# Attention and a gated MLP on one core: three edits to the order of work around the first MLP chunks

## The chip, the core and the metric

The kernel runs on one core of one Trainium2 chip. The metric is device time in microseconds, from a timed run of the whole program. The core has TensorE (PE in the profile, with its weight loads as PEld), VectorE (DVE), ScalarE (ACT), GpSimd (POOL) and SyncE (SP), which issues most of the reads from DRAM. Each engine executes its own instructions strictly in the order in which the program was written out for it.

## The reference

One layer of a transformer in float32: layer norm, attention over eight positions at distance two, a residual, layer norm, a gated MLP, a residual. Sequence 2048, model width 576, 32 heads of width 18, hidden width 4608.

```python
x = A_x
h = x + _A_ref(_layernorm(x, axis=-1), A_wqkv, A_wo)
h2 = h + _B_ref(_layernorm(h, axis=-1), B_w_gate, B_w_up, B_w_down)
...
off = jnp.arange(W) * dil                      # W = 8, dil = 2
idx = pos[:, None] - off[None, :]
logits = jnp.einsum("bhsd,bhswd->bhsw", q, kg) * scale
attn = _softmax(jnp.where(mask, logits, -1e9), axis=-1)
o = jnp.einsum("bhsw,bhswd->bhsd", attn, vg)
...
h = _sigmoid(g) * u                            # g = x @ w_gate, u = x @ w_up
return jnp.einsum("bsf,fd->bsd", h, w_down)
```

## The kernel before, in words

**Numbers.** Every float32 product is made of three products in a faster 32-bit format: an operand is split into a high half (copied by ScalarE, line 104) and a low half (the difference, by VectorE, line 105). The last 64 of the 576 model columns are handled as a "rest" of 128 rows, with a split of its own (lines 108 and 109).

**Blocks and stages.** The 2048 positions are four blocks of 512, two of even and two of odd positions, since attention steps by two. The first stage makes layer norms, transposes and the QKV projections of all blocks in four groups of eight heads (`qkv`, four tiles of 128 positions each, 14 matmuls a tile through `tok_major`, lines 157 to 160) and writes q, k and v to DRAM. Attention runs wholly on VectorE, by block and head group: `attention` reads q, a window of k (kw) and one of v (vw), multiplies (line 189) and reduces (line 193) twice for the logits, makes the softmax, then multiplies with v (line 215) and adds (lines 221, 223, 226) twice. The kw and vw tiles share three buffers. For block 1 the output is written to DRAM by GpSimd (line 228) and read back later by `load_j` (line 707).

**The front.** When the attention of block 0 is done (line 428 copies the rest columns of its output), the generator `front` brings block 0 through the output projection, the second layer norm and the transposes. Its four tiles of positions advance together, a step for each `next(fr)`: main transposes (line 146) and their splits; rest transposes (line 150) and theirs; two steps of projection (`tok_major` with wo, the sum at line 262); the norm; transposes again. Its PSUM tiles come from `any_bank`: of eight in turn, the first, second and eighth are of the tag "mm" (three buffers), the others of the tag "acc" (five buffers), which the QKV tiles use too. So the main transposes take two mm and two acc, the rest transposes three acc and one mm. Around these steps stand the last QKV tiles (blocks 2 and 3, group 3), as work for TensorE in the meantime. Before the change two steps are placed behind the second tile of block 2:

```python
    last = passes[-1]
    with tc.issue_after(getattr(last, "ins", last)):
        for _ in range(2):
            next(fr)
```

**The chunks.** The MLP has 36 chunks of 128 hidden columns for each half of the blocks. Chunks 0 to 11 of the first half are plain (`single`): a gate product in one PSUM bank (pg), a sigmoid by ScalarE (line 793), an up product in another (pu), their product by VectorE (line 766), split into halves (h0h, h0l) for the down projection (line 864, tile dp), whose results are added into a stage tile (lines 872 and 874). From chunk 12 on, `pair` computes two blocks with seven products in the place of eight; it needs the second block's operands, and their sums and differences (`sums`, lines 281 to 289, split at 105). PSUM has here three banks b1 to b3, one called bgp, and two dp tiles of two banks. Plain chunks use b1 and b2; block 1's projection, running beside later chunks, uses b3 and bgp in turn (`bg_bank`).

**Beside the chunks.** `bg_step` advances a background generator a few steps in each chunk: first the attention of block 1 (`under_first`, `att_all`), then its projection (`proj_scr`), then the operands. The read of weights for chunk f is issued by `load_gu` (line 702) on SyncE two chunks ahead, and `behind[0]` holds the last such read.

**What sets the order.** The program text gives instructions in the order above with priorities (`high_priority`); a planner then writes each engine's queue by its own estimate of when operands and buffers are free. `issue_after(i)` holds what a block of code emits on i's engine behind i in that queue.

Of the kernel before, what the change touches and what calls it, by code (L numbers as in the profile page):

```python
# [15 lines left out]
F32 = mybir.dt.float32  # L16
# [5 lines left out]
P = 128  # L22
# [38 lines left out]
def kernel(ctx, tc, x, wqkv, wo, wmlp, out):  # L61
    nc = tc.nc
    dve, act, pool, pe, sp = nc.vector, nc.scalar, nc.gpsimd, nc.tensor, nc.sync
# [26 lines left out]
    vscr = [[dr.tile([LP + TE, CG], F32, name=f"v{e}_{g}") for g in range(NG)] for e in range(2)]  # L90
# [71 lines left out]
    behind = [None]  # L162

    def window(s, hf):
        a = s[hf * TB:hf * TB + TB, :].rearrange("(p j) c -> p (j c)", p=P)
        return bass.AP(tensor=a.tensor, offset=a.offset, ap=[[NS * CG, P], [1, (NS + LP) * CG]])

    def attention(at, b, g, o):
        e, hf = BLOCKS[b]
        q = at.tile([P, NS, CG], F32, name="q")  # L170
        kw = at.tile([P, NS + LP, CG], F32, tag="kv", bufs=3, name="kw")
        vw = at.tile([P, NS + LP, CG], F32, tag="kv", bufs=3, name="vw")
        with ExitStack() as pin:
            if (b, g) == (1, 3):
                pin.enter_context(tc.issue_after(getattr(behind[0], "ins", behind[0])))
            sp.dma_start(q.rearrange("p j c -> p (j c)"), qscr[b][g])
            sp.dma_start(kw.rearrange("p j c -> p (j c)"), window(kscr[e][g], hf))
            sp.dma_start(vw.rearrange("p j c -> p (j c)"), window(vscr[e][g], hf))
        lg = sm.tile([P, NS, W, HG], F32, bufs=1, name="lg")

        def both(t, u):
            a = t[:, 2 * u:2 * u + 2]
            return bass.AP(tensor=a.tensor, offset=a.offset,
                           ap=[list(a.ap[0]), [CG, 2], [CG, W], [1, CG]])

        for u in range(2):
            us = slice(2 * u, 2 * u + 2)
            pr = at.tile([P, 2, W, CG], F32, name="pr")
            dve.tensor_tensor(pr, both(kw, u), q[:, us].unsqueeze(2).broadcast_to([P, 2, W, CG]),  # L189
                              ALU.mult)  # L190
            yield
            yield
            dve.tensor_reduce(lg[:, us].rearrange("p j w h -> p (j w h)"),  # L193
                              pr.rearrange("p j w (h d) -> p (j w h) d", d=DH),
                              AX.X, ALU.add)
            yield
        if hf == 0:
            dve.tensor_tensor(lg, lg, mask.unsqueeze(3).broadcast_to([P, NS, W, HG]), ALU.add)
        mx = sm.tile([P, NS, HG], F32, name="mx")
        rs = sm.tile([P, NS, HG], F32, name="rs")  # L200
        dve.tensor_reduce(mx, lg.rearrange("p j w h -> p j h w"), AX.X, ALU.max)
        dve.tensor_tensor(lg, lg, mx.unsqueeze(2).broadcast_to([P, NS, W, HG]), ALU.subtract)
        act.activation(lg, lg, AF.Exp, scale=SCALE)
        yield
        dve.tensor_reduce(rs, lg.rearrange("p j w h -> p j h w"), AX.X, ALU.add)
        dve.reciprocal(rs, rs)
        dve.tensor_tensor(lg, lg, rs.unsqueeze(2).broadcast_to([P, NS, W, HG]), ALU.mult)
        yield
        spill = o is None
        if spill:  # L210
            o = kw[:, 0:NS]
        for u in range(2):
            us = slice(2 * u, 2 * u + 2)
            pr = at.tile([P, 2, W, CG], F32, name="pr")
            dve.tensor_tensor(  # L215
                pr.rearrange("p j w (h d) -> p j w h d", d=DH),
                both(vw, u).rearrange("p j w (h d) -> p j w h d", d=DH),
                lg[:, us].unsqueeze(4).broadcast_to([P, 2, W, HG, DH]), ALU.mult)
            yield
            yield  # L220
            dve.tensor_tensor(pr[:, :, 0:4], pr[:, :, 0:4], pr[:, :, 4:8], ALU.add)  # L221
            yield
            dve.tensor_tensor(kw[:, 0:2 * NS].rearrange("p (k j) c -> p j k c", k=2)[:, us],
                              pr[:, :, 0:2], pr[:, :, 2:4], ALU.add)
            yield
        dve.tensor_tensor(o, kw[:, 0:NS], kw[:, NS:2 * NS], ALU.add)
        if spill:
            pool.dma_start(oscr[b][:, :, g * CG:(g + 1) * CG], o)
            if g == NG - 1:
                pool.dma_start(oscr[b][:, :, D:DX], o[:, :, CG - DR:CG])  # L230
# [165 lines left out]
    def qkv(b, g, T, w):  # L396
        e, hf = BLOCKS[b]
        ev = ev_tile([P, 3, NS, CG])
        for j in range(NS):
            ps = acc_tile()  # L400
            passes.append(tok_major(ps, NQ, *T, slice(j * P, (j + 1) * P), w[:, 0], w[:, 1]))
            with tc.high_priority(HI):
                act.activation(ev[:, :, j], ps[:, :NQ].rearrange("p (t c) -> p t c", t=3), AF.Copy)
            yield
        r0 = LP + hf * TB
        with tc.high_priority(HI):
            act.dma_start(qscr[b][g], ev[:, 0].rearrange("p j c -> p (j c)"))
            for t, s in ((1, kscr), (2, vscr)):
                act.dma_start(s[e][g][r0:r0 + TB, :].rearrange("(p j) c -> p (j c)", p=P),
                              ev[:, t].rearrange("p j c -> p (j c)"))  # L410
        emitted.add((b, g))
# [188 lines left out]
    def front():  # L600
        ar = tok_tile((P, 5, TB))
        oT = th_tile(), tl_tile()
        gens = []
        for j in range(NS):
            js = slice(j * P, (j + 1) * P)

            def put(pv, cs, js=js):
                if not X:
                    X["a00"], X["a01"] = tl_tile(), th_tile()
                if cs.start == 0:  # L610
                    for t, c in ((X["a00"], 0), (X["a01"], 2)):
                        split(t[:, 0:2, js], t[:, 2:4, js], pv[:, c:c + 2])
                else:
                    split_rest(X["a01"][:, 4, js], pv[:, 0])
                act.activation(ar[:, cs, js], pv, AF.Copy)

            gens.append(proj_j(any_bank, (o[:, j], h[:, j]), wos, oT[0][:, :, js], oT[1][:, :, js],
                               lambda j=j: o[:, j], put, (1, 0)))
        k = 0
        while gens:  # L620
            with tc.high_priority(HI):
                gens = [gn for gn in gens if next(gn, END) is not END]
            k += 1
            if k == 4:
                act.dma_start(hacc[0], h)
            yield
        act.dma_start(xscr[0], ar)
# [13 lines left out]
    fr = front()  # L641
# [10 lines left out]
        step(ag, 1)  # L652
    last = passes[-1]
    with tc.issue_after(getattr(last, "ins", last)):
        for _ in range(2):
            next(fr)
    for b in (2, 3):
        for j, _ in enumerate(more if b == 2 else qkv(b, 3, T[b], w[3])):
            with ExitStack() as way:
                if (b, j) == (2, 0):  # L660
                    way.enter_context(tc.issue_after(getattr(passes[-1], "ins", passes[-1])))
                next(fr, END)
            step(ag, 1)
        if b == 2:
            with tc.high_priority(2 * HI):
                wg = xt.tile([P, WC], F32, tag="tl", bufs=4, name="wg0")
                sp.dma_start(wg, wmlp[0])
                ww = first_split(wg)
# [22 lines left out]
    gp = ctx.enter_context(ps_pool("gp"))  # L691
# [81 lines left out]
    def b_tile(i):  # L773
        return gp.tile([P, TB], F32, name=f"b{i % 3 + 1}")
# [6 lines left out]

    def single(X, w, t, units, side):
        xa, xb = (X["a00"], X["a01"]) if t == 0 else (X["a10"], X["a11"])
        pg, pu = b_tile(0), b_tile(1)
        prod(pg, xa, w, "b00", True)
        side(0)
        if c == NSTD - 3:
            units(1)
        prod(pg, xb, w, "b10", False)
        rest(pg, xb, w, "g4")  # L790
        sg = s_tile()
        with tc.high_priority(HC):
            act.activation(sg, pg, AF.Sigmoid)
        side(1)
        units(1)
        side(2)
        prod(pu, xa, w, "b01", True)
        side(3)
        prod(pu, xb, w, "b11", False)
        rest(pu, xb, w, "u4")  # L800
        with tc.high_priority(HC):
            hid = hidden(sg, pu, f"h{t}")
        side(4)
        if c != NSTD - 3:
            units(1)
        side(5)
        return {t: hid}
# [238 lines left out]
    c = 0  # L1046
# [201 lines left out]
    for c, (kind, p, f) in enumerate(items):  # L1248
        w, d = wc
        for b, late_c in ((0, NF + NSTD - 3), (1, NF + NSTD + 5)):  # L1250
            if c == late_c:
                e, hf = BLOCKS[b]
# [115 lines left out]
```

## Time and profile before

| | |
|---|---|
| device time, median of three | 1581.74 us (1579.36 to 1583.03) |
| the profiled execution | 1584.01 us |
| span of that execution, first to last instruction | 1582.2 us |
| busy: PE, DVE, ACT, POOL | 1551.0, 1255.2, 879.2, 199.9 us |
| attention in DVE's groups from 220 to 309 us: lines 189, 193, 215 | 10.2 us each |

Times in the profile count from the first instruction of the span. A line of the timeline gives start, duration, engine, line, operation, output and inputs, the count of merged instructions, and in brackets the idle time before them with what ended it ("<-DVE tok L428": an instruction of VectorE at line 428). In the waits, "PE mm L150 <- DVE tok L428: 1.7, 1, 1.7" says that TensorE's line 150 waited for that in total 1.7 us, once, at longest 1.7. SPq rows are reads that SyncE issues; their time is that of the issue, not of the transfer. The front lies at 179 to 220 us, plain chunks follow from 220.49, and the first pair chunk begins at 357.73.

### The profile page before, as it was taken

Reading aid. Unit: us, or ns where it says so; the run is one execution under the profiler, and the core shown is the slowest. Engines: PE = TensorE matmul, PEld = TensorE weight load, DVE = VectorE, ACT = ScalarE, POOL = GpSimd, SP = SyncE. Lnnn points to the kernel's source line nnn. Section 1 sums busy time; section 2 is a strip of 40 time slices with the busy share of each in tenths; the row PEclk is TensorE's granted clock in tenths of the full one; section 3 lists DMA queues with packets and bytes.
Section 4 is the critical chain, followed back from the end, with each engine's and each line's share of the span. In section 5 each row is a group of like instructions: output and inputs, shape, how many; then the busy total and the mean of one; then the engine's idle time right before and its main releaser. Section 6 shows DMA issues by size and latency. Waiting matters only on the chain.

```text
span 1582.2 us, 22347 instructions
## 1 busy us (share of the span) xinstructions
PE 1551.0 (98%) x8520; PEld 1377.3 (87%) x8520; DVE 1255.2 (79%) x1883; ACT 879.2 (56%) x1584; POOL 199.9 (13%) x249
## 2 busy tenths in 40 slices
PE   8999999999999999999999999999999999999998
PEld 7999888887888888888888888888888888888887
DVE  6998999969999999999426588866777776677755
ACT  6632244435555645566542355766777766777660
POOL 2300000020000010000101010112112112111210
PEclk9999999999999999999999999999999999999999
DMA  8646445365566677664683524999899989999983
GB/s 284 215 168 220 179 185 190 108 235 183 133 167 170 164 176 192 157 162 109 161 242 125 181 81 126 193 181 177 170 180 186 173 173 181 173 173 186 181 169 120
DMA packets 77147, 273.95 MB, mean 173 GB/s; under 512 B 8336, under 2 KB 14224, under 8 KB 76144
## 3 DMA queue, kind: packets, MB, share of 16 engines
q0 software_dynamic: 28192, 107.29, 37.5%
q1 hardware_dynamic: 41216, 145.11, 27.2%
q10 hardware_dynamic: 7632, 20.12, 3.3%
q8 instruction: 66, 1.08, 0.3%
q14 instruction: 41, 0.34, 0.1%
HBM read 143.98 MB, written 130.87 MB: 174 GB/s over the span
## 4 chain that ended last, share of the span: by engine, by line
PE 58%; issue 16%; DVE 11%; DMA 8%; POOL 4%; ACT 2%; SPq 0%; ACTq 0%; POOLq 0%; DVEq 0%
PE b L746 27%; PE dp L864 13%; PE dp L926 6%; PE b L753 5%; PE acc L157 4%; POOL h L935 3%; DMA wg<-in_wmlp_dram 3%; DVE pr L189 2%; DVE pr L215 1%; DVE lg L193 1%; DVE w L105 1%; DVE pr L221 1%; PE b L157 1%; PE bgp L157 1%; DMA x<-tok 1%
## 5 line engine op out<-in xcount | busy, mean ns | idle before, releaser
L746 PE MATMUL b<-tl,w 128*128 128x512 f32 x1704 | 432.6, 393 | 5.1 <-ACT s L820 3.2
L746 PEld LDWEIGHTS b<-tl,w 128*128 128x128 f32 x1704 | 307.9, 188 | 63.6 <-ACT s L820 4.7
L746 PE MATMUL b<-th,w 128*128 128x512 f32 x1344 | 346.2, 392 | 1.5 <-DVE s L839 1.5
L746 PEld LDWEIGHTS b<-th,w 128*128 128x128 f32 x1344 | 244.8, 188 | 46.5 <-DVE s L839 1.9
L932 ACT ACTIVATE ev<-dp 128x576 f32<-128x576 f32 x224 | 144.7, 646 | 63.2 <-PE dp L926 58.9
L753 PE MATMUL b<-th,w 128*128 128x512 f32 x568 | 175.7, 390 | 0.0
L104 ACT ACTIVATE w<-wg 128x384 fp32r<-128x384 f32 (+1 forms) x186 | 110.8, 601 | 111.1 <-PE b L753 48.8
L935 POOL DMA_DIRECT2D h<-ev x128 | 110.0, 860 | 458.6 <-ACT ev L932 444.7
L157 PE MATMUL acc<-qw,th 128*128 128x432 f32 x512 | 154.3, 362 | 2.5 <-DVE th L109 2.3
L105 DVE TENSOR_TENSOR w<-wg,w 128x640 fp32r<-128x640 f32 (+1 forms) x186 | 120.8, 656 | 41.3 <-ACT w L104 41.1
L105 DVE TENSOR_TENSOR w<-tw,w 128x512 fp32r<-128x512 f32 x120 | 82.6, 688 | 82.1 <-ACT w L104 81.5
L753 PEld LDWEIGHTS b<-th,w 128*128 128x128 f32 x568 | 106.5, 188 | 23.2
L864 PE MATMUL dp<-d,h1h 128*128 128x288 f32 x640 | 119.9, 297 | 0.0
L864 PE MATMUL dp<-d,h0h 128*128 128x288 f32 x608 | 114.1, 297 | 0.8 <-DVE tail L874 0.8
L872 ACT ACTIVATE stage<-dp 128x576 f32<-128x576 f32 x104 | 66.9, 645 | 70.1 <-PE dp L864 69.8
L157 PEld LDWEIGHTS acc<-qw,th 128*128 128x128 f32 x512 | 96.6, 189 | 8.4 <-DVE th L109 3.5
L864 PEld LDWEIGHTS dp<-d,h1h 128*128 128x128 f32 x640 | 99.7, 190 | 3.0
L104 ACT ACTIVATE w<-tw 128x512 fp32r<-128x512 f32 x120 | 75.4, 628 | 46.5 <-PE b L746 40.0
L864 PEld LDWEIGHTS dp<-d,h0h 128*128 128x128 f32 x608 | 95.1, 190 | 4.3 <-DVE tail L874 1.0
L157 PE MATMUL acc<-qw,tl 128*128 128x432 f32 x256 | 92.6, 362 | 0.1
L189 DVE TENSOR_TENSOR pr<-kw,q 128x2304 f32<-128x2304 f32 x32 | 81.8, 2556 | 8.8 <-DMA kw<-k 8.7
L880 POOL DMA_DIRECT2D h<-stage x26 | 31.0, 1194 | 436.3 <-ACT stage L872 350.1
(310 smaller groups left out, 2955.5 us busy)
## 6 DMA issues: line engine op xcount, KB each, us to landing
h<-ev POOLq DMA_DIRECT2D x96, 576.0 KB, 7.1
wg<-in_wmlp_dram SPq DMA_DIRECT2D x47, 928.0 KB, 5.9
h<-stage POOLq DMA_DIRECT2D x26, 1152.0 KB, 9.5
wg<-in_wmlp_dram SPq DMA_DIRECT2D x36, 640.0 KB, 4.3
kw<-k SPq DMA_DIRECT2D x16, 792.0 KB, 5.2
vw<-v SPq DMA_DIRECT2D x16, 792.0 KB, 4.3
wd<-in_wmlp_dram SPq DMA_DIRECT2D x18, 576.0 KB, 7.4
h<-ev POOLq DMA_DIRECT2D x32, 288.0 KB, 6.9
```

What stands on the lines that cost most here:

```text
L104: act.activation(hi, src, AF.Copy)
L105: splits.append(dve.tensor_tensor(lo, src, f32(hi), ALU.subtract))
L157: pe.matmul(ps[:, :n], a[:, c, js], m[:, c], start=k == 0, stop=False)
L189: dve.tensor_tensor(pr, both(kw, u), q[:, us].unsqueeze(2).broadcast_to([P, 2, W, CG]), ALU.mult)
L746: pe.matmul(ps, wt[:, a, k0 + c], xx[:, m + c], start=first and k == 0, stop=k == 5, skip_group_check=True)
L753: pe.matmul(ps, wt[:, a, k0], xx[:, 4], start=False, stop=a == 1, skip_group_check=True)
L864: pe.matmul(ps[:, i, :DH2], a[:, js], d[:, m, i * DH2:(i + 1) * DH2], start=k == 0, stop=k == n)
L872: act.activation(hv, ps, AF.Copy)
L880: pool.dma_start(hacc[b], hs, accum_op=ALU.add, max_dma_last_dim=8 * D)
L926: pe.matmul(ps[:, i, :DH2], a[x][:, js], m[y], start=k in (0, 1, 3) and q == 0, stop=q == 2, skip_group_check=True)
L932: act.activation(hs[:, k % 2], ps[:, :, :DH2], AF.Copy)
L935: pool.dma_start(hsev[:, u, k0:k + 1], hs[:, :k + 1 - k0], accum_op=ALU.add, max_dma_last_dim=8 * D)
```

## The change

Three edits.

In `attention`, for block 1 and head group 2 alone, the read of vw is not issued with those of q and kw, but after the second reduction of the logits (line 193) and behind the last weight read that has been issued up to there. By the order of the program text that reduction falls in chunk 1, so that read is chunk 3's, the second that `load_gu` issues.

In the front, only the main transposes stay behind the second QKV tile of block 2. The rest transposes come behind the third tile, and after them the first projection step as before.

In `single`, chunks 1, 3 and 5 of the first half accumulate in b3 and bgp in place of b1 and b2.

```diff
@@ attention
             sp.dma_start(q.rearrange("p j c -> p (j c)"), qscr[b][g])
             sp.dma_start(kw.rearrange("p j c -> p (j c)"), window(kscr[e][g], hf))
-            sp.dma_start(vw.rearrange("p j c -> p (j c)"), window(vscr[e][g], hf))
+            if (b, g) != (1, 2):
+                sp.dma_start(vw.rearrange("p j c -> p (j c)"), window(vscr[e][g], hf))
...
                               AX.X, ALU.add)
+            if (b, g, u) == (1, 2, 1):
+                with tc.issue_after(getattr(behind[0], "ins", behind[0])):
+                    sp.dma_start(vw.rearrange("p j c -> p (j c)"), window(vscr[e][g], hf))
             yield
@@ the front
     with tc.issue_after(getattr(last, "ins", last)):
-        for _ in range(2):
-            next(fr)
+        next(fr)
     for b in (2, 3):
         for j, _ in enumerate(more if b == 2 else qkv(b, 3, T[b], w[3])):
             with ExitStack() as way:
                 if (b, j) == (2, 0):
                     way.enter_context(tc.issue_after(getattr(passes[-1], "ins", passes[-1])))
+                    next(fr)
                 next(fr, END)
             step(ag, 1)
@@ single
-        pg, pu = b_tile(0), b_tile(1)
+        if t == 0 and c < 6 and c % 2:
+            pg, pu = b_tile(2), gp.tile([P, 512], F32, name="bgp")
+        else:
+            pg, pu = b_tile(0), b_tile(1)
```

## The prediction, made before the changed kernel ran

> **What bounds the kernel now.** I read the busy times first, then TensorE's (PE's) waits, the busy time by stage and the chain of waits, and last the timelines of PE, VectorE (DVE) and SyncE around the places that the diff touches.
>
> ```profile
> span 1582.2 us, 22347 instructions
> PE 1551.0 (98%) x8520; PEld 1377.3 (87%) x8520; DVE 1255.2 (79%) x1883; ACT 879.2 (56%) x1584; POOL 199.9 (13%) x249
> ```
>
> PE is busy for 98% of the span, so the whole change plays for the little that PE is idle. All three edits lie between 178 and 376 us. Of PE's waits in that stretch the longest is for a reload of attention output (4.23 us, its row stands below); the next are these (total, times, longest):
>
> ```profile
> PE mm L150 <- DVE tok L428: 1.7, 1, 1.7
> PE acc L157 <- DVE th L109: 1.6, 1, 1.6
> PE dp L864 <- DVE h0l L105: 0.9, 1, 0.9
> ...
> PE dp L864 <- ACT h0h L104: 0.2, 1, 0.2
> ```
>
> The 1.7 and 1.6 stand where the QKV tile is moved, the 0.9 and 0.2 in the plain chunks, and none at the v read. What a wait of PE is worth depends on who else is full. Busy time by stage (length, then PE, PEld, DVE, ACT, POOL, granted PE clock, DMA):
>
> ```profile
> 189.00:308.00 119.00, 117.39 (x654) 103.80 (x653) 113.14 (x160) 51.29 (x97) 3.94 (x6) 1.00 0.42 151
> 308.00:325.00 17.00, 12.77 (x58) 11.17 (x58) 7.59 (x12) 5.76 (x10) 1.45 (x2) 0.80 0.69 241
> 316.00:325.00 9.00, 5.58 (x25) 5.38 (x26) 2.76 (x5) 2.14 (x4) 0.00 (x0) 0.62 0.84 300
> ```
>
> From 189 to 308 us DVE is nearly as full as PE (113.1 of 119 us against 117.4): the attention of block 1 runs on it under the plain chunks. From 308 to 325 it has 17 − 7.6 = 9.4 us of idle time. How the two engines are tied, the chain of waits shows:
>
> ```profile
> 307.86 0.68 DVE kw L226
> ...
> 309.46 6.85 DMA o<-kw
> ```
>
> The last attention sum of block 1 (L226) ends at 308.5; its write to DRAM lands 6.85 us after its issue, the rows are read back, and only then does PE get them. In PE's timeline:
>
> ```profile
> 319.42 1.11 PE L146 MATMUL b<-ident,oj 128*128 128x128 f32 x4 [4.23 <-DMA oj<-o]
> ...
> 365.60 1.56 PE L746 MATMUL b<-tl,w 128*128 128x512 f32 x6
> ```
>
> and in DVE's:
>
> ```profile
> 364.39 1.22 DVE L105 TENSOR_TENSOR tl<-ar,tl 128x1024 fp32r<-128x1024 f32 x1
> ```
>
> The projection that starts at 319.42 ends in the operands of the first pair chunk. DVE ends the split of one of them at 365.61, and PE uses it at 365.60: it follows at DVE's heels. So a microsecond that PE wins at 180 is kept only so far as DVE's chain to these splits gets earlier too. The numbers stand on that.
>
> **The QKV tile between the transposes.** PE's order now (start, length, in brackets the idle time before):
>
> ```profile
> 179.39 0.71 PE L146 MATMUL mm<-ident,tok 128*128 128x128 f32 x5
> 181.79 0.33 PE L150 MATMUL mm<-ident,tok 128*128 128x128 f32 x1 [1.70 <-DVE tok L428]
> ...
> 182.29 0.71 PE L146 MATMUL acc<-ident,tok 128*128 128x128 f32 x5
> 182.84 0.49 PE L150 MATMUL acc<-ident,tok 128*128 128x128 f32 x3
> ...
> 185.30 0.46 PE L157 MATMUL acc<-qw,th 128*128 128x432 f32 x1 [1.65 <-DVE th L109]
> ...
> 188.14 0.29 PE L157 MATMUL mm<-wo,th 128*128 128x288 f32 x1
> ```
>
> A rest transpose stands among the main ones and waits 1.70 us for the copies of L428. The QKV tile stands last and waits 1.65 us for an accumulator from which a rest transpose is still being read. With the tile in between, no rest transpose can precede it, and the five "acc" tiles hold two older QKV tiles, two main tiles and this one, so it should find one free. Then PE's 16 main transposes at 0.11 (five from 182.29 to 182.84) end at 181.15; the tile takes 188.14 − 185.30 = 2.84, to 183.99; four rest transposes end at 184.4. The projection follows when DVE has made the low halves:
>
> ```profile
> 181.65 2.55 DVE L193 TENSOR_REDUCE lg<-pr 128x128 f32<-128x2304 f32 x1
> ...
> 184.95 0.71 DVE L109 TENSOR_TENSOR th<-acc,th 64x128 fp32r<-64x128 f32 x3
> ...
> 186.51 1.28 DVE L105 TENSOR_TENSOR tl<-acc,th 128x512 fp32r<-128x512 f32 x2
> 187.70 2.55 DVE L189 TENSOR_TENSOR pr<-kw,q 128x2304 f32<-128x2304 f32 x1
> ```
>
> With the reduction still first (to 184.2) and the four main halves (0.64 each) ahead of a rest half (0.24), the projection starts at 187.0 instead of 188.14: PE gains 1.1. If the halves come before the reduction, or the next QKV tile fills the hole, both waits go: 3.35. If the rest halves fall behind the product at 187.70 (2.55), it starts near 190.5: a loss of 2.4. I take 2.2, the middle of the first two, since the new order of PE leaves DVE time for the main halves while the tile runs.
>
> What DVE gets from it is less. Two of its waits before 308 are PE's doing, directly or through ScalarE, which in turn was held by the write of the transposed block that follows the projection:
>
> ```profile
> 227.15 0.69 DVE L766 TENSOR_TENSOR s<-s,b 128x512 f32<-128x512 f32 x1 [1.25 <-PE b L753]
> ...
> 232.99 0.83 DVE L105 TENSOR_TENSOR w<-wg,w 128x640 fp32r<-128x640 f32 x1 [0.55 <-ACT w L104]
> ```
>
> ```profile
> 231.16 0.69 ACT L104 ACTIVATE d<-wg 128x576 fp32r<-128x576 f32 x1 [1.94 <-DMA x<-tok]
> ```
>
> With PE 2.2 us ahead both close: 1.25 + 0.55 = 1.8. Besides, a PE that is ahead brings chunk work of DVE forward. Its groups from 220 to 309 us (busy us after the bar) make 14.5 + 9.0 + 6.2 + 6.2 + 5.9 = 41.8 us:
>
> ```profile
> L105 DVE TENSOR_TENSOR w<-wg,w 128x640 fp32r<-128x640 f32 (+2 forms) x25 | 14.5, 608 | 1.7 <-ACT w L104 1.7
> ...
> L874 DVE TENSOR_TENSOR stage<-stage,dp 128x576 f32<-128x576 f32 x12 | 9.0, 751 | 0.3 <-PE dp L864 0.3
> L105 DVE TENSOR_TENSOR h0l<-s,h0h 128x512 fp32r<-128x512 f32 x9 | 6.2, 685 | 0.0
> L766 DVE TENSOR_TENSOR s<-s,b 128x512 f32<-128x512 f32 x9 | 6.2, 684 | 1.4 <-PE b L753 1.2
> L105 DVE TENSOR_TENSOR d<-wg,d 128x576 fp32r<-128x576 f32 x8 | 5.9, 745 | 0.0
> ```
>
> That is 0.47 us for each us of the stage, so 2.2 us bring 1.0 us forward. What lands in DVE's idle 9.4 us shortens the time to the later splits; what lands before 308 delays the attention by as much. I count half, 0.5, between 0 and 3.35 × 0.47 = 1.6.
>
> **The banks.** Chunks 1, 3 and 5 accumulate in b3 and bgp, so neighbours share no bank and PE need not wait for the gating product (L766) of the chunk before. But PE's waits in the plain chunks, the 0.9 and 0.2 above, are of a down projection for a hidden half, not for a bank. I count 0, between a gain and a loss of 1.1. The two banks' other user, block 1's projection, starts at 319.42, after the odd chunks.
>
> **The v read.** On SyncE's queue it stands ahead of the weight reads:
>
> ```profile
> 216.88 0.32 SPq L178 DMA_DIRECT2D vw<-v  x1
> 217.29 20.66 SPq L702 DMA_DIRECT2D wg<-in_wmlp_dram  x3
> ...
> 243.62 0.33 SPq L702 DMA_DIRECT2D wg<-in_wmlp_dram  x1
> ...
> 254.11 0.33 SPq L702 DMA_DIRECT2D wg<-in_wmlp_dram  x1
> ```
>
> Its time to landing on the page (KB, median us), and its reader:
>
> ```profile
> vw<-v SPq DMA_DIRECT2D x16, 792.0 KB, 4.3
> ```
>
> ```profile
> 248.11 2.56 DVE L215 TENSOR_TENSOR pr<-vw,lg 128x2304 f32<-128x2304 f32 x1
> ```
>
> Behind two weight reads at 0.41 us each (216.88 to 217.29) it leaves at 217.7 and lands at 222.0; DVE wants it at 248.11. So the move costs nothing as long as the read stays ahead of 243.6. The weight reads can leave earlier, but no wait above names them: 0, and at most the 0.55 counted already.
>
> Sum: 1.8 + 0.5 + 0 + 0 = 2.3 us less. The profiled execution took 1584.01 us beside its span of 1582.2, which gives 1581.7; the three times shown have a median of 1581.74, which gives 1579.4.
>
> **The rivals.** 0.2% is 3.2 us, about what a measurement of this kernel can tell from no change.
>
> Given back: PE wins its 2 us and stands that much longer at 319.42, or at the splits near 365, because DVE is no earlier. For it speaks how little idle time DVE has; against it the 1.25 us that name PE. It gives 1581.7.
>
> More than forecast: the order comes out so that the wait at 319.42 shrinks and the clock holds. From 316 to 325 the clock averages 0.62; at half speed that is 2 × 0.38 × 9 = 6.8 us, of which about 5.2 lie behind 319.42 and cost 2.6. With the 2.3 that makes 4.9 less: 1576.8. With all 1.6 of work brought forward and the 1.1 of the hidden halves it is 7.1: 1574.6. By how much the wait must shrink the trace leaves open, since a wait of 1.95 us was also followed by a slow stretch (0.63):
>
> ```profile
> 835.96 0.66 PE L146 MATMUL b<-ident,oj 128*128 128x128 f32 x4 [1.95 <-DVE tl L105]
> ```
>
> ```profile
> 837.00:841.00 4.00, 4.00 (x22) 4.00 (x21) 2.18 (x3) 0.99 (x2) 0.00 (x0) 0.63 1.00 395
> ```
>
> [...]
>
> Slower: the v read comes too late. It is now written out only after the second logit reduction, in chunk 1, so the planner may set it behind later weight reads. Behind the one at 243.62 it lands at 248.3, and there the cost begins. Behind that of 254.11 it lands at 258.8, 10.7 us late; DVE can fill 10.7 × 0.47 = 5.0 of that with chunk work, so the attention, the reload and the pair operands slip by 5.7, and what the front won is lost in the same wait: 1587.4. Against it: its buffer is free at 216.88, and up to 243 the queue has few other reads.
>
> **How the numbers follow.** Forecast 0.47 (its own range 1577.5 to 1581.5; 0.13 of it beyond 3.2 us, 0.34 within), given back 0.15 (0.12 within, 0.03 slower by a new wait), more than forecast 0.25 (0.24 faster, 0.01 within), v read late 0.13 (0.12 slower, 0.01 within). Faster 0.37, same 0.48, slower 0.15. The range goes from the second rival's end, 1574.6, to half of the last one's price, 1584.6.
>
> **What would show it.** Right: no wait of L150 for L428 and none of a QKV tile for L109; the projection's first matmul 1 to 3 us earlier; DVE's wait before the first L766 gone; the last L226 of block 1 ending 1 to 2 us earlier; the v read behind two weight reads, and no wait of L215 for it. Wrong: the front's gain there and the first pair chunk not earlier, or the wait for oj longer by the same amount; a clock below 1.00 near 185; changed waits after 400 us, of which the sum has none.

## The result, and the profile after

The changed kernel takes 1587.44 us (median of 6 runs, 1587.06 to 1588.02) against 1582.12 us for the kernel before in the runs beside it (6 runs, 1577.12 to 1583.03). The ratio is 1.0039, with a 95% interval from 1.0021 to 1.0058; in a second set of runs it was 1.0047 (1.0029 to 1.0065). So it is slower, by about 6 us. The prediction had 1579.4 us in a range that ended at 1584.6.

The head of the page after:

```profile
span 1586.1 us, 22341 instructions
PE 1551.2 (98%) x8520; PEld 1378.1 (87%) x8520; DVE 1256.4 (79%) x1883; ACT 880.4 (56%) x1584; POOL 200.1 (13%) x249
```

PE is busy as long as before (1551.2 us against 1551.0), and its stretches at half clock are as long in sum (10.2 us in both without the program's last microseconds, but in other places), so nearly all of the 3.9 us by which the span grew is idle time of PE. PE's waits from 170 to 450 us, in total, times, longest:

```profile
PE b L750 <- ACT s L837: 3.9, 1, 3.9
PE b L750 <- ACT s L827: 2.4, 1, 2.4
PE acc L150 <- DVE tl L105: 2.1, 1, 2.1
PE b L750 <- DVE s L846: 1.6, 1, 1.6
PE b L750 <- DVE w L105: 0.9, 1, 0.9
PE b L146 <- DMA oj<-o: 0.9, 1, 0.9
```

(Lines behind the first edit stand 1 to 7 lower than before: 190 was 189, 750 was 746, 837 was 830, 230 was 226, 887 was 880.) Where they lie, PE's timeline shows:

```profile
185.44 0.33 PE L150 MATMUL acc<-ident,tok 128*128 128x128 f32 x1 [2.13 <-DVE tl L105]
...
320.58 0.66 PE L146 MATMUL b<-ident,oj 128*128 128x128 f32 x4 [0.89 <-DMA oj<-o]
...
381.64 2.93 PE L750 MATMUL b<-tl,w 128*128 128x512 f32 x6 [3.90 <-ACT s L837]
...
421.11 1.66 PE L750 MATMUL b<-th,w 128*128 128x512 f32 x6 [1.57 <-DVE s L846]
432.04 4.15 PE L750 MATMUL b<-tl,w 128*128 128x512 f32 x10 [2.44 <-ACT s L827]
```

The waits of a rest transpose for L428 and of a QKV tile for L109 are gone, and a new one of 2.13 us stands in their place. The wait for the reload fell from 4.23 to 0.89 us. Between 377 and 432 us, in pair chunks that no edit touches, three waits of 3.90, 1.57 and 2.44 us are new. The kernel before has a single long one from 370 to 440 us, and it is gone after:

```profile
393.31 4.65 PE L746 MATMUL b<-tl,w 128*128 128x512 f32 x18 [2.37 <-ACT s L820]
```

How the start of PE's n-th matmul moved tells what each was worth. The 800th starts 0.95 us earlier than before (there is no edit ahead of it yet, so a microsecond is chance here), the 1000th (198 us before) 0.90 earlier, the 1600th (311 us) 0.35 later, the 1800th 4.5 earlier, the 1900th (366.5 us before, 360.8 after) 5.74 earlier, the 2400th (463 us) 3.4 later and the 3000th 5.1 later. So in this execution the front won nothing, the reload won 5 us, and 9 us went between the 1900th and the 2400th. The busy time in the stretch from 360 to 440 us, before and after (length, then PE, PEld, DVE, ACT, POOL, granted PE clock, DMA):

```profile
360.00:440.00 80.00, 77.19 (x406) 66.46 (x405) 76.25 (x100) 42.96 (x71) 4.40 (x4) 1.00 0.53 145
```

```profile
360.00:440.00 80.00, 72.09 (x355) 60.58 (x354) 66.02 (x90) 39.94 (x66) 8.32 (x10) 0.96 0.53 156
```

That is 5.1 us less busy time of PE, and two stretches of 3.41 us at half clock (381.2 and 432.4 us), worth 1.7 us each.

**Where the wait at 377.7 begins.** ScalarE's timeline, before and after:

```profile
374.53 1.15 ACT L104 ACTIVATE w<-wg 128x384 fp32r<-128x384 f32 x2 [1.17 <-PE b L753]
```

```profile
378.76 0.74 ACT L104 ACTIVATE w<-wg 128x640 fp32r<-128x640 f32 x1 [4.48 <-DMA wg<-in_wmlp_dram]
...
381.01 0.57 ACT L837 ACTIVATE s<-b 128x512 f32<-128x512 f32 x1
```

After, the splitting of chunk 14's weights waits 4.48 us for their read, and behind it in ScalarE's queue stands the copy (L837) that empties the bank PE wants. SyncE issues that read at almost the same time in both:

```profile
369.77 0.33 SPq L702 DMA_DIRECT2D wg<-in_wmlp_dram  x1
```

```profile
368.66 0.33 SPq L706 DMA_DIRECT2D wg<-in_wmlp_dram  x1
```

It can't leave sooner, although PE is 5.74 us ahead: its buffer is free when DVE ends the split of chunk 12's down weights, at 369.70 before and 368.60 after. The DMA view has the median time to landing of the same read, before and after (KB, us):

```profile
wg<-in_wmlp_dram SPq DMA_DIRECT2D x1, 928.0 KB, 4.8
```

```profile
wg<-in_wmlp_dram SPq DMA_DIRECT2D x1, 928.0 KB, 10.1
```

The reason is on GpSimd's queue, before and after:

```profile
348.95 4.28 POOL L1055 DMA_DIRECT2D h<-z  x6 [0.30 <-POOL z L1052]
378.51 1.24 POOL L880 DMA_DIRECT2D h<-stage  x1 [25.28 <-DVE stage L874]
```

```profile
366.50 1.26 POOL L887 DMA_DIRECT2D h<-stage  x1 [17.84 <-DVE stage L881]
...
368.41 4.28 POOL L1062 DMA_DIRECT2D h<-z  x6 [0.30 <-POOL z L1059]
```

The write that adds the sums of chunks 0 to 11 to DRAM (1152 KB) left 8.7 us behind the read before, and leaves 2.2 us ahead of it after. It came forward by 12 us because the planner now has 22 more matmuls of the plain chunks ahead of the first transpose of the reloaded rows (1639 matmuls from the start to there, 1617 before). These 22 are also what covers the reload: in the six profiles of this case with 1639 matmuls ahead of it PE waits 0.3 to 1.4 us there, in the ten with 1617 2.9 to 4.6 us. Gain and loss are two ends of one change of order.

### The profile page after: what moved, and what is told of

Read it like the earlier page. It is cut to its first block, busy times and chain, and to the rows that moved or that the text cites. A ratio compares the mean times of both kernels' runs of the same rounds, so it can differ in the third digit from the quotient of the medians.

```text
span 1586.1 us, 22341 instructions
## 1 busy us (share of the span) xinstructions
PE 1551.2 (98%) x8520; PEld 1378.1 (87%) x8520; DVE 1256.4 (79%) x1883; ACT 880.4 (56%) x1584; POOL 200.1 (13%) x249
## 3 DMA queue, kind: packets, MB, share of 16 engines
q0 software_dynamic: 28192, 107.29, 37.4%
## 4 chain that ended last, share of the span: by engine, by line
PE 38%; issue 28%; DVE 15%; DMA 9%; POOL 7%; ACT 2%; POOLq 0%; ACTq 0%; SPq 0%; DVEq 0%
PE b L750 16%; PE dp L871 10%; POOL h L942 7%; DMA wg<-in_wmlp_dram 5%; PE acc L157 4%; PE b L757 3%; DVE w L105 2%; DVE lg L194 2%; DVE pr L190 2%; DVE pr L219 2%; PE b L157 1%; PE bgp L157 1%; DVE pr L225 1%; DVE s L770 1%; DMA x<-tok 1%
## 5 line engine op out<-in xcount | busy, mean ns | idle before, releaser
L105 DVE TENSOR_TENSOR w<-wg,w 128x384 fp32r<-128x384 f32 (+1 forms) x186 | 120.6, 654 | 41.6 <-ACT w L104 41.1
```

Source lines behind the costliest of these rows:

```text
L105: splits.append(dve.tensor_tensor(lo, src, f32(hi), ALU.subtract))
```

## The experiments

Two theories stood at the start. A: the changed kernel has a head start of 5 us and loses it on the late weight reads of chunks 14 and 16. B: the banks' order of chunks is itself what loses. From the second set on, A was split: C, the read lands late because of the accumulating write ahead of it; D, only the late release of its buffer counts. All ratios are to the kernel before on the same chip, with their 95% intervals.

**The three edits alone.** First the front:

```diff
     with tc.issue_after(getattr(last, "ins", last)):
-        for _ in range(2):
-            next(fr)
+        next(fr)
...
                     way.enter_context(tc.issue_after(getattr(passes[-1], "ins", passes[-1])))
+                    next(fr)
                 next(fr, END)
```

> Only the front edit: the rest transposes stand behind the third QKV tile; banks and v read as before. Theory A (the head start is lost on late weight reads: PE reaches the second and later pair chunks early, but the reads of their weights start only when the low half of an earlier chunk's down weights has been made, which is not earlier): PE gains 1 to 3 us by 200 us, loses the wait for oj only in part, and gives the gain back between 375 and 435 us; 1581 to 1585. Theory B (the loss comes from one edit's own new order, and it is that of the banks): no loss after 375 us, 1578 to 1581.

Measured: 1584.83 us, 1.0017 (1.0002 to 1.0032). The front edit alone loses. At the front PE waits 1.86 us for the third rest transpose, with half clock behind it, as in the changed kernel; more lies in the plain chunks. SyncE, ScalarE and PE:

```profile
223.60 0.32 SPq L178 DMA_DIRECT2D vw<-v  x1
224.01 18.09 SPq L702 DMA_DIRECT2D wg<-in_wmlp_dram  x3
```

```profile
235.34 0.74 ACT L104 ACTIVATE w<-wg 128x640 fp32r<-128x640 f32 x1 [4.93 <-DMA wg<-in_wmlp_dram]
```

```profile
236.61 0.73 PE L746 MATMUL b<-tl,w 128*128 128x512 f32 x2 [2.61 <-ACT s L793]
```

With the front edit the v read leaves 6.7 us later than before and still stands ahead of the weight reads; ScalarE waits for weights, and PE for the sigmoid behind it. The time lies in theory A's range, but not for A's reason: PE is not ahead at the 1900th matmul (1.4 us later than before), and its only long wait from 370 to 445 us is one of 2.51 us near 392, as the kernel before has.

Then the banks:

```diff
-        pg, pu = b_tile(0), b_tile(1)
+        if t == 0 and c < 6 and c % 2:
+            pg, pu = b_tile(2), gp.tile([P, 512], F32, name="bgp")
+        else:
+            pg, pu = b_tile(0), b_tile(1)
```

> Only the banks of plain chunks 1, 3 and 5. Theory A: PE comes ahead by some us in the plain chunks, the wait for oj (4.23 us before) shrinks, and the waits between 375 and 435 us grow from the 2.4 us of before to 5 us or more: 1582 to 1588. Theory B: the whole loss, 1586 to 1589, also where PE is not ahead at 360 us.

Measured: 1579.17 us, 0.9993 (0.9976 to 1.0010). No gain or loss that can be told, and none of the three new waits; the one near 391 us of the kernel before is there (2.67 us at 386). Theory B falls. What theory A expected of this run did not come either: PE is 4.7 us ahead at the 1900th matmul, and the waits did not grow to 5 us. Here the read of chunk 14 leaves 4.7 us sooner as well, at 365.06, and the accumulating write stays 8.7 us behind it: a head start alone loses nothing.

Then the v read:

```diff
-            sp.dma_start(vw.rearrange("p j c -> p (j c)"), window(vscr[e][g], hf))
+            if (b, g) != (1, 2):
+                sp.dma_start(vw.rearrange("p j c -> p (j c)"), window(vscr[e][g], hf))
...
+            if (b, g, u) == (1, 2, 1):
+                with tc.issue_after(getattr(behind[0], "ins", behind[0])):
+                    sp.dma_start(vw.rearrange("p j c -> p (j c)"), window(vscr[e][g], hf))
```

> Only the v read behind the first weight reads. Both theories: the first weight read leaves some 20 us earlier (near 195 us instead of 217 us), no wait of L219 for v, PE's waits as before, 1581 to 1583. If the v read is the cause by itself: 1585 or more with a longer wait for oj.

Measured: 1581.74 us, 0.9997 (0.9983 to 1.0011): nothing, alone.

**The weight reads brought forward.** The changed kernel, with the split of the down weights put first where chunks 12 to 14 are prepared, so that their buffers come free earlier:

```diff
-            split(d[:, 0], d[:, 1], wd)
+            with ExitStack() as way:
+                if c in (11, 12, 13):
+                    way.enter_context(tc.high_priority(HI))
+                split(d[:, 0], d[:, 1], wd)
```

> The changed kernel, with one addition: the split of the down weights of chunks 12, 13 and 14 is planned at high priority, so that the buffer of the weights comes free some 8 to 12 us earlier and the reads for chunks 14, 15 and 16 leave earlier. Theory A: the waits of PE at 377.7 (3.9 us), 419.5 (1.6) and 429.5 (2.4) and the two stretches of half clock behind them go, and the head start of 5.75 us stays: 1575 to 1579, faster than before. Theory B: no change or a random one, 1584 to 1590.

Measured: 1578.43 us, 0.9979 (0.9964 to 0.9994), 9 us less than the changed kernel. The read of chunk 14 leaves at 354.96 us, that of chunk 16 at 391.45; the accumulating write is still there at 365.28, but now behind the read. The stretch from 360 to 440 us:

```profile
360.00:440.00 80.00, 78.22 (x406) 66.46 (x406) 75.10 (x101) 46.54 (x77) 9.33 (x12) 1.00 0.59 174
```

PE does 6.1 us more in it than in the changed kernel, and the clock holds. The control is the same edit in the kernel before:

> Control for the run that put the split of the down weights of chunks 12 to 14 forward in the changed kernel (1578.4 us): the same put forward in the kernel before, without the three edits. Theory A (the changed kernel loses its head start on late weight reads alone): in the kernel before only the wait of 2.37 us at 390.9 us belongs to these weights, so the gain is at most about 2.4 us plus a little of its slow clock: 1578.5 to 1581.5, and TensorE's 1900th matmul starts at most 2 us earlier. Rival (the split put forward is itself what gained 9 us, with the edits or without): about 1573 to 1575.

Measured: 1577.82 us, 0.9989 (0.9977 to 1.0001). This is below the expected 1578.5, but by the ratio it gains at most 3.6 us, not 9. In its profile the 1800th matmul comes 5.3 us earlier, which was not expected either; that lies ahead of the edit's place, 3.4 us of it at the reload, where this execution waited 2.94 us at full clock and the profile of before 4.23 with half clock behind it. So the split put forward is worth little in the kernel before and about the whole loss in the changed one, as A has it. With the split in both, 0.9979 and 0.9989, the three edits make no difference that the intervals can tell.

**The changed kernel without its front edit** (the diff of the first experiment, reversed):

> The changed kernel without its front edit: the banks and the v read alone. Theory A: with the banks alone (1579.2) the late reads did not hurt, and the v read alone did nothing, so 1578 to 1580.5, and no wait of TensorE over 2 us between 370 and 385 us. Rival (the v read, harmless alone, does harm beside the banks): 1584 or more.

Measured: 1580.46 us, 1.0007 (0.9995 to 1.0019). The banks and the v read together do nothing.

**Collision or late release.** The changed kernel without the first accumulating write of block 0:

```diff
-            if j == NS - 1 and n == NSTD // 2 - 1:
+            if j == NS - 1 and n == NSTD // 2 - 1 and b:
                 add_dram(b, hs)
```

> The changed kernel without one transfer: the accumulating write of the stage tile of block 0 after chunks 0 to 11 is left out, so the sums of these chunks are missing in the output for that block. Theory C (collision: the weights of chunk 14 leave at 368.7 us in both kernels, and land late in the changed one only because that write of 1152 KB was issued 2.2 us ahead of them): the read still leaves within 2 us of 368.7 and its first user starts 5 to 6 us later instead of 10; TensorE's wait of 3.89 us at 377.7 us and the slow clock behind it go; those at 419 and 429 stay; 1581 to 1584. Rival D (the late release of the buffer alone, the write has no part): the wait at 377.7 stays over 3 us, and the time stays within 2 us of 1587.

Measured: 1581.46 us, 1.0009 (0.9994 to 1.0023), some 5 us below the changed kernel. The read of chunk 14 leaves at 368.97, as late as ever, and lands as in the kernel before; ScalarE waits for PE, not for it:

```profile
wg<-in_wmlp_dram SPq DMA_DIRECT2D x1, 928.0 KB, 4.8
```

```profile
374.06 1.15 ACT L104 ACTIVATE w<-wg 128x384 fp32r<-128x384 f32 x2 [1.01 <-PE b L757]
```

The wait at 377.7 us is gone, and those of chunk 16 stay (1.64 and 2.41 us). D would have kept the first. One thing moves beside the write: the six zero writes (288 KB each), no longer behind it on GpSimd's queue, go at 349.64 us as in the kernel before. At chunk 16 there are no zero writes, and there the second write was left out too:

```diff
-            if j == NS - 1:
+            if j == NS - 1 and not (b == 0 and c == NSTD + 2):
                 add_dram(b, hs)
```

> As the run without the first accumulating write, and the next one of block 0 is left out too (the write at 407.8 us, just ahead of the weights of chunk 16), so those sums are missing as well. Theory C: the waits at 419.5 (1.57 us) and 429.5 (2.44 us) and their slow clock go too: 1576 to 1580. Rival D: they stay, and the time is within 2 us of the run with one write left out.

Measured: 1576.42 us, 0.9976 (0.9963 to 0.9989), another 5 us less. The weights of chunk 16 are used 10.3 us after their issue with one write left out (404.13 to 414.44), and 5.05 us after it with two (406.78 to 411.83). By the stretch from 360 to 440 us, one write left out and two:

```profile
360.00:440.00 80.00, 75.95 (x387) 64.68 (x387) 71.24 (x96) 43.33 (x72) 3.20 (x3) 0.98 0.46 141
```

```profile
360.00:440.00 80.00, 79.94 (x428) 69.51 (x428) 76.38 (x105) 47.10 (x78) 2.00 (x2) 1.00 0.42 140
```

PE goes from 72.09 to 75.95 to 79.94 us busy of 80. C holds, and at chunk 16 one accumulating write ahead of the read was enough for it. Whether a write of this size that doesn't accumulate would do the same was not tried.

**What the front edit is worth with the reads on time.** The banks, the v read and the split put forward, without the front edit:

> The changed kernel with the split of the down weights of chunks 12 to 14 put forward and without the front edit: beside the run with all three edits and that split forward (1578.4 us, ratio 0.9979) it leaves out the front edit alone. Theory F1 (the QKV tile between the transposes neither wins nor loses once the weight reads are on time; its loss in the run of the front edit alone was late work further on): 0.997 to 0.999, 1576 to 1579. Theory F2 (the front edit itself costs about 2.7 us, as its run alone gave): 0.995 to 0.9965, 1573 to 1575.

Measured: 1578.10 us, 0.9974 (0.9960 to 0.9987), beside 0.9979 with the front edit. That lies in F1's range: no gain or loss of the front edit can be told here. The interval reaches below 0.9965, so F2 isn't quite excluded. The same without the v read:

> The banks and the split put forward, in the kernel before: no front edit, and the v read where it was. If the v read is harmless here too, the same as the run with it, within 0.1%: 1576 to 1579 by theory F1, 1573 to 1575 by theory F2. This or the run beside it is the version that should beat both kernels.

Measured: 1579.56 us, 0.9988 (0.9975 to 1.0001). The two intervals overlap. The first of them has the lowest ratio of the kernels that compute the whole layer; the changed kernel with the split put forward (0.9979) can't be told from it.

**Both kernels profiled once more.**

> The changed kernel once more, beside these two, and with a second profile of it. If the collision of the accumulating write with the weight read is a property of the order of instructions and not of one execution: TensorE waits again over 3 us near 377 us and over 1.5 us near 420 and 430, and the ratio to before is 1.002 to 1.006. If it was chance, these waits are gone and the profiled span is under 1582. Separately, on the clock: in all profiles so far TensorE's half clock comes in stretches of 3.41 us that lie on one grid in an execution, and follows a cell of the grid with over 1.85 us of idle time; by that, whether the wait for the third rest transpose near 183 us costs 1.7 us more depends on how it falls on the grid.

Measured: 1588.55 us, 1.0047 (1.0029 to 1.0065), span 1587.6 us, with the same waits in PE's timeline:

```profile
383.50 2.28 PE L750 MATMUL b<-tl,w 128*128 128x512 f32 x6 [3.72 <-ACT s L837]
...
424.09 1.97 PE L750 MATMUL b<-th,w 128*128 128x512 f32 x6 [1.98 <-DVE s L846]
```

The collision belongs to the order of instructions. The wait near 430 us was smaller than expected, 0.90 us at 434. The third rest transpose waited 2.62 us, from 185.15 to 187.77, and no half clock followed, where the wait of 2.13 us in the first profile had it. By the spacing of PE's matmuls, two half-clock stretches of this profile end near 387.7 and 428.6; steps of 3.41 us counted back from there put a limit near 186.3, an estimate, and that parts the wait into some 1.2 and 1.5 us.

> A second profile of the kernel before. In the run with only the split of chunks 12 to 14 put forward, TensorE's order up to 363 us was the same as here, yet its wait for the reload near 316 us was 2.94 us, not 4.23, and no half clock followed. If such differences are from one execution to the next: the wait comes out anywhere between 2.9 and 4.6 us here, and 0 to 2 half-clock stretches follow it. If they belong to the kernel: 4.0 to 4.5 us and two stretches.

Measured: one run, 1582.77 us; the wait for the reload is 4.11 us, and half clock follows for two stretches. The second reading, that this belongs to the kernel, is not shown by that: with PE's order the same up to there, the runs of the banks, of banks and v read, and of the split put forward in the kernel before had 3.01, 3.02 and 2.94 us, others 4.25 and 4.6. The write of the attention output landed in 5.5 to 5.6 us in those of the first kind and in 6.9 in the kernel before and with the v read alone. What decides between the two stays open; it moves a run by 1 to 3 us.

**The two pairs with the front edit.**

> The front edit and the v read, without the banks. Two things are open. First, what the v read does beside the front edit: with the front edit alone the v read left at 223.60 us, just ahead of two weight reads that took 11.8 us to land, ScalarE waited 4.93 us for them and TensorE 2.61 us behind it. If that is the price, both waits are gone here and the ratio is at least 0.0015 below the 1.0017 of the front edit alone, unless the second thing happens: the planner puts 22 more matmuls ahead of the reload (1639 in place of 1617), the accumulating write leaves near 366 us, just ahead of the weights of chunk 14, and TensorE waits over 3 us near 378 us, with a ratio of 1.003 to 1.005. If the banks are needed for that order: 1617 matmuls, the write later than 372 us, no such wait, 0.998 to 1.001.

Measured: 1582.31 us, 1.0011 (0.9999 to 1.0023); 1617 matmuls ahead of the reload, the write at 377.33. SyncE's queue now has weight reads at 194.52 us and near 217, the v read behind them at 221.99, and ScalarE has no wait for weights up to 240 us. The wait that the front edit brought is gone, as expected; of the 0.0015 only 0.0006 shows, which these intervals can't tell from either.

> The front edit and the banks, the v read where it was. If the v read in the way of the weight reads is the price of the front edit, ScalarE waits over 3 us for weights near 235 us again, and TensorE over 1.5 us behind it. If the front edit and the banks are the pair that makes the order with 1639 matmuls ahead of the reload, the write leaves near 366 us and the wait near 378 us is over 3 us: 1.004 to 1.007. If the v read is needed for that order: 1617 matmuls, no such wait, 1.000 to 1.003.

Measured: 1587.18 us, 1.0042 (1.0026 to 1.0057); 1639 matmuls ahead of the reload, the write at 368.84, PE's waits of 3.78, 1.49 and 2.45 us back in the pair chunks. And the v read is in the way again:

```profile
234.15 1.46 ACT L104 ACTIVATE w<-wg 128x640 fp32r<-128x640 f32 x3 [3.49 <-DMA wg<-in_wmlp_dram]
```

So front and banks are the pair that makes the new order, and with it the collision: either without the other has 1617 matmuls and a write no earlier than 373.79 us.

## Why the prediction was wrong, point by point

**What bounds the kernel.** Right that PE is full and that a lead counts only so far as what follows is ready. The chain was followed to the first pair operands at 365.6 and not further. The step that failed for the time is there: the sum puts nothing behind it, with "changed waits after 400 us, of which the sum has none" left as a sign of error. The trace of before held that term. The read of chunk 14, issued at 369.77, landed 4.8 us later, and ScalarE used it from 374.96 on: it had 0.4 us of slack, and its release hung on DVE. Besides, the write of 1152 KB left as soon as DVE's last sum was done, only 8.7 us behind that read. A change of order ahead of these two could swap them, and did: the read then took 10.1 us to land. The price is 5.1 us of PE's work and 3.4 of clock in the 80 us from 360.

**The QKV tile.** The waits for L428 and L109 went, as said, and in this profile the gain of 2.2 us was not there. "It should find one free" was right for the QKV tile, but five acc tiles were then held by it, two older ones and two main tiles, and the next three rest transposes asked for acc as well. The third took a main tile's, from which DVE was still reading (the row at 185.44). The prediction's four rest transposes with no wait between them are the step that failed in the front. DVE's rest halves fell behind the product, its downside case:

```profile
185.90 2.54 DVE L190 TENSOR_TENSOR pr<-kw,q 128x2304 f32<-128x2304 f32 x1
188.48 0.71 DVE L109 TENSOR_TENSOR th<-acc,th 64x128 fp32r<-64x128 f32 x3
```

The projection did not wait for them: its first twelve matmuls (line 157) take the main halves alone, and only the two behind them (lines 159 and 160) the rest. So its first matmul came at 185.63 instead of 188.14, 2.5 us earlier (0.95 of it was there ahead of the edits) and so within "1 to 3", but it ran on at half clock (0.50 from 186.62 to 190.03), which the prediction had named as a sign of error, and at the 1000th matmul nothing was left. One profile does not settle what the front is worth. From the 800th matmul to the 1000th the eight profiles with the front edit take 34.9 to 38.9 us (mean 36.3), the eight without it 36.3 to 39.4 (mean 37.4), the kernel before 36.8 and the changed one 36.85. The wait for the third rest transpose is in all eight, from 1.28 to 2.64 us; the edit wins about 1 us in the mean, which is no more than the two profiles of the kernel before differ by (36.8 and 38.0).

**DVE's 1.8 and 0.5.** The wait of 1.25 us ahead of L766 went, and one of 1.71 us for ScalarE's h0h came 5 us later. Block 1's last attention sum was to end 1 to 2 us earlier:

```profile
309.84 0.75 DVE L230 TENSOR_TENSOR kw<-kw 128x576 f32<-128x576 f32 x1
```

Before, it started at 307.78. It is 2 us later, and that term has the wrong sign. From 189 us to the end of that sum DVE is idle 7.15 us, and 5.86 before; and eight splits of down weights stand ahead of it in place of seven (0.75 us each). These 1.29 and 0.75 are the 2 us: the waits grew, where the prediction had them close, and chunk work moved ahead of the attention.

**The banks.** 0 was right in time for the edit alone. What was missed is that it changes the planner's order: with the front edit, 22 more matmuls stand ahead of the reload.

**The v read.** It leaves at 222.33, behind two weight reads, and its reader waits for nothing:

```profile
194.86 22.62 SPq L706 DMA_DIRECT2D wg<-in_wmlp_dram  x2
222.33 0.33 SPq L199 DMA_DIRECT2D vw<-v  x1
```

```profile
249.67 2.56 DVE L219 TENSOR_TENSOR pr<-vw,lg 128x2304 f32<-128x2304 f32 x1
```

So the rival "v read late" did not come true, although its 1587.4 us lie next to the result. Saying that "no wait above names" the weight reads was right for the kernel before and not beside the front edit: in the two runs that have the front edit without this move, ScalarE waited 4.93 and 3.49 us for them. In time the move shows nothing that the intervals can tell (1.0011 beside 1.0017, 1.0039 beside 1.0042).

**More than forecast.** This rival came true in its place: the wait at 319.42 shrank and the clock held there, worth 5 us from the 1600th matmul to the 1800th, where 4.9 was said. That the numbers agree is luck: the 4.9 were 2.3 from the front and DVE, which did not come, and 2.6 of clock. It came by more chunk work ahead of the reload, not by a head start, and it was lost from 377.7 us on.

## What to carry to other kernels

Where a planner writes the queues, an edit that costs nothing where it stands can still swap two transfers 200 us later, so list the transfers of the stages that follow, with the slack of each read (landing against first use), and the large writes that are ready close to one (here 1152 KB, issued 8.7 us behind the read before and 2.2 us ahead of it after). Here the lead was kept when the reads behind it left sooner too: they hung on a split in DVE's queue, and putting that split first turned the change from 1.0039 into 0.9979, beside 0.9989 for the kernel before with the same split. When counting buffers for a reordered step, count on to the last step that takes from the same ring, not only to the one that was moved.

## What the runs showed of the hardware

**A read behind an accumulating write.** The profile counts the packets of the read and of the write against the same 16 DMA engines. What the two kinds of queue moved in the changed kernel in the 8 us from 366, around the read's issue at 368.66 (packets, MB, share of the engines; software is GpSimd's, hardware SyncE's):

```profile
q0 software_dynamic: 208, 0.96, 69.8%
q1 hardware_dynamic: 23, 0.17, 5.3%
```

The write, issued at 366.50, moved packets from 368.33 on and landed at 377.06. The read's first packet moved at 372.98, 4.3 us after its issue (1.0 in the kernel before, where no packet of such a write moved between 364 and 380 us), and its 128 packets then took 5.2 us (3.5 before). Why it stood still for the first 4.3 us, the profile does not show.

**Half clock and PE's idle time.** In the profiles of the kernel before and of the changed one, without the first 13 us, for which they have no clock, and the last stretch, which runs to the program's end, the granted clock is 0.50 from 317.73 us for 6.83 and from 836.55 for 3.41 (before), and from 186.62, 381.18 and 432.38 for 3.41 each (after). Within each execution the starts lie a whole number of 3.41 us apart (152 of it before, 57 and 15 after), so each has a grid of its own; counted from the start of the span, the one after lies 2.0 us further on. In the cell of this grid ahead of a stretch PE was idle for 2.53 and 1.95 us (before) and for 2.13, 3.41 and 2.44 us (after). The most that a cell at full clock held with no half clock behind it was 1.87 us (389.40, before) and 1.79 us (838.57, after). Of the cells at half clock, one with 1.69 us was followed by another (317.73, before) and one with 0.46 us was not (381.18, after). The front of the changed kernel, one cell and the next, and the reload in the kernel before with the split put forward, three stretches of the same length:

```profile
183.21:186.62 3.41, 1.28 (x10) 1.18 (x10) 3.38 (x6) 1.24 (x5) 0.00 (x0) 1.00 0.98 411
186.62:190.03 3.41, 3.41 (x17) 3.41 (x16) 2.74 (x5) 1.46 (x3) 0.00 (x0) 0.50 0.16 33
```

```profile
311.58:315.00 3.42, 1.71 (x9) 1.25 (x7) 1.64 (x3) 1.79 (x3) 0.00 (x0) 1.00 0.41 106
315.00:318.41 3.41, 2.17 (x17) 2.02 (x18) 0.81 (x2) 1.11 (x2) 0.00 (x0) 1.00 1.03 363
318.41:321.82 3.41, 3.41 (x20) 2.50 (x21) 2.87 (x5) 1.86 (x5) 0.00 (x0) 1.00 1.00 414
```

The wait of 2.13 us fell into one cell, and the 3.41 us at half clock behind it cost 1.7 us more. The one of 2.94 us is spread over two stretches (1.71 and 1.24 us), and the clock stayed at 1.00. So the length of a wait alone did not decide whether the prediction's "2.6 us of clock" came on top. That it is where the wait falls on the grid, which differed between the two profiles above, is the author's reading; no run varied that alone.
